# New times, priorities, load order and one engine choice for a chained attention, expert and channel-mix kernel

## The chip, the cores and the metric

The kernel runs on one core of a Trainium2 chip. The metric is device time in microseconds (us) of one execution; the profile shows one such execution of the kernel before. TensorE is called PE below, VectorE DVE, ScalarE ACT, GpSimd POOL, and SyncE SP; SP issues the transfers (DMAs).

## What is computed

Three layers follow each other, all in float32 (8 batches, 576 positions, width 512):

```python
p_packed = sm_attn(p, k, v)              # 32 packed queries look at 576 keys, 8 heads of 64
out = sm_attn(q, p_packed, p_packed)     # 576 queries look at the 32 packed rows
...
for e in range(E):                       # 4 experts, causal attention of width 64, top 2 by gate
    q = x @ wq[e]; k = x @ wk[e]; v = x @ wv[e]
    ...
    ye = a @ v @ wo[e]
    out += mask[..., None] * w[:, :, kk:kk + 1] * ye
...
xk = mu_k * x + (1.0 - mu_k) * x_prev    # x_prev: x shifted by one position
xr = mu_r * x + (1.0 - mu_r) * x_prev
k = np.maximum(xk @ w_k, 0.0)
v = k * k @ w_v
r = 1.0 / (1.0 + np.exp(-(xr @ w_r)))
return (r * v)
```

## The kernel before

**Precision.** A float32 product is made of three products of tiles that are split into a high and a low part (names ending in h and l): high by high, low by high, high by low.

**Phases.** From 0 to about 387 us the kernel runs the attention and the experts, batch after batch, and beside it folds the experts' output weights `wo` into the last layer's weights `w_r` and `w_k` (function `fold`, lines L693 to L791): each weight piece arrives as 64-bit words (`raw`), DVE, ACT and POOL turn it to float32 (`decode`), PE multiplies it (L777), and the folded weights go to DRAM (`wscr`). Of the four planes of a folded weight only two are stored; the other two are rebuilt when it is loaded. From 387 us `rstage` (L944) computes the r gate, from 459 us `kstage` (L964) the hidden layer, from 589 us `vunit` (L1005) the last product.

**What rebuilds a weight.** `load_weight` loads the two stored planes of `wr` (near the end of the expert phase), of `wk0` and of `wk1` (during `rstage`). For each of the two missing planes it subtracts (L864, 128x1024, into the single buffer `ws`), rounds to the high part on ACT (L865), and subtracts again for the low part on DVE (L866). The stored planes are split at L850 to L853.

**Steps and their times.** Each part of the work is a generator whose pieces ("steps") get a time from a table, in units of which a batch has 20: `front` (attention), `values`, `project` (L474, L487, L493: q, k of two experts), `soft` (L539 scores, L557 mask and row maximum on DVE, L561 exponential on ACT), `turn` (L586, L593: transposes), `pair_out` (L616 to L663: probabilities by values at L628, scaling `cs`, `cx`, `cb`, and `dt`, which goes to DRAM), `fold`, and the loads and stages of the last layer. The steps are sorted by time and written out in that order; a scheduler then fixes each engine's queue, with priorities (`PR`, `PR0`, `PR1`) that let a step's instructions go ahead. On the chip every engine works its queue strictly in order, and so does SP, on whose queue all DMAs stand: an instruction that waits holds all behind it.

**Shared buffers.** PSUM tiles come from two pools: `one` has four buffers, `big` two. A matmul into a `big` tile waits until the readers of the tile two before it are done. DMAs use eight semaphores in rotation, so each waits for the one eight before it. DMA `ms<-ms` (L570) moves the 64x64 corner `mq` of an expert's scores between the buffers, and L593 transposes it.

**The opening.** `load_first` issues the first loads in the order of `LOADS` (`k`, `v`, `q` with the head group, `wo`, `r` for a raw weight piece, `wa` for the experts' input weights). `FILL` adds 128x64 matmuls that only keep PE working.

Of the kernel before, what the change touches and what calls it, by code (L numbers as in the profile page):

```python
# [20 lines left out]

FRONT_T = [-29.98, -26.81, -23.33, -16.88, -17.51, -14.04, -12.67, -12.1, -8.35]
G1_T = [1.16, 2.59, 3.23, 1.72, 1.63, 8.19, 3.77, 1.61, 3.2]
OPEN_T0 = [-29.98, -26.81, -23.33, -16.88, -17.51, -14.04, -12.67, -12.1, -8.35]
OPEN_T1 = [-28.82, -24.22, -20.1, -15.16, -15.88, -5.85, -8.9, -10.49, -5.15]
VAL_T = [-3.35, 0.36, -1.9, 0.35, 0.62]
PROJ_T = [-2.04, -1.82, 1.38, 2.56]
GROUPS = ((0, 3), (1, 2), (4,))  # L30
SOFT_T = [1.76, 1.75, 2.48]
TURN_LAG = [4.78, 4.58, 5.02]
OUT_LAG = [3.59, 5.08, 7.48]
FOLD_0 = [-21.99, -18.2, -16.87, -12.45, -10.56, -6.17, -3.87, -1.05, -0.52, 1.63, 3.63, 7.17, 8.98]
FOLD_T = [5.65, 105.86]
LOADS = 'k0 k1 v0 q0 wo r r v1 q1 wa'
LATE1 = [0.0, 0.0]
TIES_V, TIES_A = [0, 1, 2, 2], [0, 0, 1, 1]
FILL = [[0, 0, 0, 0, 0, 0], [0, 0, 0, 0, 0, 0]]
Q_MOVE = 'SSSS'  # L40
SLOTS = 2
E_SLOT = 'V'
E_HALF = 'D'
SMALL0 = 'VV'
SEQ = ''
PR0, WARM = (1000, 946, 1043, 1073, 1037, 1000, 940, 980, 907), 16
PR1 = [990, 936, 1033, 1063, 1027, 990, 930, 970, 897]
WR_AT = 7.41
R_LOAD, R_RUN = ([15.69, 16.11], [22.66, 28.61])
W_AT = [5.5, 5.2]  # L50
K_AT = [(0, -1.0, 0)] + [(0, 0.0, j) for j in range(4)] + [(1, -1.0, 0)] + [(1, 0.0, j) for j in range(5)]
E_TURN = "VAAAA"
E_DIAG = "AAAAV"
E_TURN2 = "AAAAA"
E_DIAG2 = "AAAVA"
E_WH, E_SQ, E_B, E_G, E_CXL = "P", "A", "V", "V", "A"
E_AT, E_VG, E_CB, E_PT, E_PPT, E_CX = "A", "A", "A", "V", "A", "V"
E_Z = "P"
E_DT, E_WL = "P", "P"
PR = {'front': 0, 'values': -100, 'project': 0, 'soft': 0, 'turn': 0, 'out': 236, 'fold': 0, 'k': 46, 'gates': 0}  # L60


def f32(ap):
    return ap.bitcast(F32)
# [3 lines left out]
def kernel(  # L68
# [83 lines left out]
    if True:  # L152
# [41 lines left out]
        def zeros():  # L194
            for t in kls:
                nc.gpsimd.memset(f32(t[64:, 0, :]), 0.0)
                nc.gpsimd.memset(f32(t[:64, 1, :]), 0.0)
            yield
            for x, t in enumerate(mss):
                nc.gpsimd.memset(t, 0.0)  # L200
                if x < len(tbs):
                    nc.gpsimd.memset(rowap(tbs[x][64:, :64], TS + P, NT, 64), 0.0)
                yield

        def halves(ap):
            return ap.rearrange("p (h n) -> p h n", h=2)
# [4 lines left out]
        def evac(eng, o, x):  # L211
            if eng == "A":
                return nc.scalar.copy(o, x)  # L213
            if eng == "V":
                return nc.vector.tensor_copy(o, x)
            return pool_copy(o, x)
# [56 lines left out]
        def load_first():  # L273

            got = {}
            first["raw"] = []
            for x in LOADS.split():
                if x == "wa":
# [15 lines left out]
        def fill(b, g, x, ps, o, ins):  # L294


            for _ in range(0 if b else FILL[g][x]):
                with tc.issue_after(ins.ins):
# [162 lines left out]
        def project(b, ep):  # L461
# [5 lines left out]
            for x in range(2):  # L467
# [17 lines left out]
                if x == 0:  # L485
                    nc.scalar.copy(halves(z[:, 0, :]), pv)
                    nc.vector.tensor_sub(halves(l), pv, halves(f32(z[:, 0, :])))  # L487
                    evac(E_Z, z[64:, 1, :], f32(z[64:, 0, :]))
                else:
# [18 lines left out]
        def rowap(base, stride, n, w):  # L508
            return bass.AP(
                tensor=base.tensor, offset=base.offset, ap=[base.ap[0], [stride, n], [1, w]]  # L510
            )
# [64 lines left out]
        def turn(b, e, group):  # L576
# [17 lines left out]
            for i, o in blocks:  # L594
                if i:
                    q0 = i * P - TAIL
                    evac(
                        (E_TURN if b < 4 else E_TURN2)[i], rowap(tb[:, q0 : q0 + P], TS, i, P),
                        ps[:, o : o + i * P].rearrange("p (j q) -> p j q", q=P),
# [3 lines left out]
            evac(  # L603
                (E_DIAG if b < 4 else E_DIAG2)[i],
                rowap(tb[:64, (TS + P) * i : (TS + P) * i + 64], step, ng, 64),
# [210 lines left out]
        def call(fn, *args):  # L816
            fn(*args)
            yield
# [36 lines left out]
        def load_weight(n_, eng):  # L855
            h, l = wres[n_]
            for j in range(SLOTS):
                fetch(f32(l[:, j]), wscr[n_][:, j], True)
            yield
            sub = (nc.vector if E_SLOT == "V" else nc.gpsimd).tensor_sub  # L860
            if SLOTS < NS:
                w = pools["a"].tile([P, 2, 512], F32, tag="ws", name=nm("ws"), bufs=1)
                for j, x in ((2, l[:, 0]), (3, w)):
                    pin(sub(w, f32(x) if j == 2 else x, f32(l[:, 1])))  # L864
                    pin(nc.scalar.copy(h[:, j], w))  # L865
                    pin(nc.vector.tensor_sub(l[:, j], w, f32(h[:, j])))  # L866
                    yield
            for j in range(SLOTS):
                split_late(h[:, j], l[:, j], eng)
                yield  # L870

        def swap_end():

            close(sm_cm, vp_cm, ex_cm, bt_cm)
            cms["b"], pools["b"] = pool("bb", 1, "left")
            for n_ in ("k0", "k1"):
                weight(n_, "b")
                yield from load_weight(n_, "AV" if n_ == "k0" else "AP")
            wres["v"] = [
                pools["b"].tile([P, NFT, DM], F32R, name="wv" + x, bufs=1) for x in "hl"  # L880
            ]
            yield
# [130 lines left out]

        last = U * (B - 1) + max(t + max(0, d) for t, d in zip(FRONT_T, G1_T)) + 0.1
        prio = {}

        def add(kind, gen, times, prior=None):
            prio[gen] = PR[kind] if prior is None else prior
            for t in times:
                steps.append((t, gen))  # L1020

        def even(t0, t1, n):
            return [t0 + (t1 - t0) * i / n for i in range(n)]

        add("front", zeros(), [-6.0 + 0.5 * i for i in range(6)])
        add("fold", fold(), FOLD_0 + even(FOLD_T[0], FOLD_T[1], NFOLD - len(FOLD_0)))
        swap = max(last, FOLD_T[1] + 0.1)
        add("k", call(swap_w), [swap])
        add("k", load_weight("r", "PV"), [swap + WR_AT - 2.0] + even(swap + WR_AT + 1.0, swap + WR_AT + 5.0, 4))
        end = U * B + OUT_LAG[2] + 0.1  # L1030
        for i in range(NEB):
# [149 lines left out]
```

## Time and profile before

| | us |
|---|---|
| median of 3 runs (lowest, highest) | 795.42 (792.72, 796.65) |
| the profiled execution, own time | 790.75 |
| its span | 789.0 |
| PE busy in it | 755.3 (96%) |
| DVE, ACT, POOL busy | 478.5, 453.1, 357.7 |

The span is the time from the first to the last instruction on the core; 1.75 us of the execution's own time lie around it. PE's mean granted clock is 0.978 of full speed.

### The profile page before, as it was taken

The page shows a single profiled execution, that of the slowest core. Times are in us where ns is not written, and L with a number is a line of the kernel's source. Part 1 is how long each engine was busy: PE and PEld are TensorE (multiplying, and loading weights), DVE is VectorE, ACT ScalarE, POOL GpSimd, SP SyncE. Part 2 cuts the span into 40 slices and gives each one's busy share as a digit, 9 for nine tenths or more (in the row PEclk, how much of TensorE's full clock was granted, in tenths as well). Part 3 has the DMA queues.
Part 4 walks back from the last instruction along what each step waited for, and adds up shares of the span by engine and source line. Part 5 has one row for each costly group of instructions (what it writes and reads, how often), then busy time and mean ns, then how long its engine had stood idle before and what let it go on. Part 6 is the DMA issues. An engine that isn't in the chain of part 4 may idle for free.

```text
span 789.0 us, 15325 instructions
## 1 busy us (share of the span) xinstructions
PE 755.3 (96%) x5504; PEld 622.3 (79%) x5504; DVE 478.5 (61%) x1182; ACT 453.1 (57%) x1031; POOL 357.7 (45%) x456
## 2 busy tenths in 40 slices
PE   6788989999999999999899999999999999999998
PEld 4486967879697887877778888888888888888886
DVE  3977886988868668777757978887581111111111
ACT  2367757678767769687633442422968756555400
POOL 7357657664766715252501063631267443433600
PEclk8599999999999999999899999999999999999999
DMA  9955463545636353215358686857889565555411
GB/s 317 302 152 169 129 182 116 170 152 160 197 111 175 116 143 109 71 37 147 118 187 287 227 265 203 292 190 236 322 279 338 170 188 172 181 181 158 135 65 54
DMA packets 88460, 142.06 MB, mean 180 GB/s; under 512 B 9280, under 2 KB 60992, under 8 KB 86080
## 3 DMA queue, kind: packets, MB, share of 16 engines
q1 hardware_dynamic: 88240, 141.07, 56.3%
q8 instruction: 44, 0.72, 0.4%
q14 instruction: 32, 0.26, 0.1%
q10 hardware_dynamic: 144, 0.00, 0.0%
HBM read 83.90 MB, written 47.19 MB: 166 GB/s over the span
## 4 chain that ended last, share of the span: by engine, by line
PE 78%; DMA 7%; DVE 7%; ACT 3%; POOL 2%; issue 1%; SPq 1%; DVEq 0%; ACTq 0%; POOLq 0%
PE one L1005 25%; PE one L964 8%; PE big L964 8%; PE big L474 6%; PE one L628 5%; PE one L944 4%; PE big L944 4%; PE one L777 4%; PE one L419 3%; PE one L539 2%; PE one L586 2%; DMA raw<-in_w_k_dram 2%; DMA ms<-ms 2%; PE big L244 2%; PE big L539 1%
## 5 line engine op out<-in xcount | busy, mean ns | idle before, releaser
L1010 DVE TENSOR_TENSOR ring<-one,ring 128x512 f32<-128x512 f32 x36 | 24.9, 692 | 167.8 <-PE one L1005 158.5
L1005 PE MATMUL one<-wvh,yh 128*128 128x512 f32 x288 | 112.0, 389 | 0.0
L1005 PE MATMUL one<-wvl,yh 128*128 128x512 f32 x288 | 112.0, 389 | 0.0
L1005 PE MATMUL one<-wvh,yl 128*128 128x512 f32 x288 | 112.0, 389 | 0.0
L561 ACT ACTIVATE ms<-ms,nb 128x192 f32<-128x192 f32 (+3 forms) x128 | 78.5, 617 | 19.1 <-DVE nb L557 18.6
L219 POOL TENSOR_TENSOR yl<-yvh,yh 128x1024 fp32r<-128x1024 f32 (+1 forms) x24 | 49.1, 2060 | 44.3 <-ACT yh L990 26.3
L213 ACT COPY tb<-one 64x128 f32<-64x128 f32 (+5 forms) x208 | 61.7, 362 | 10.9 <-PE one L593 9.9
L708 POOL TENSOR_TENSOR dcx<-dcx,dcu 128x256 f32<-128x256 f32 x40 | 29.9, 747 | 83.3 <-DVE dcu L702 61.2
L1005 PEld LDWEIGHTS one<-wvh,yl 128*128 128x128 f32 x288 | 54.1, 188 | 11.3
L1005 PEld LDWEIGHTS one<-wvh,yh 128*128 128x128 f32 x288 | 54.1, 188 | 11.2
L1005 PEld LDWEIGHTS one<-wvl,yh 128*128 128x128 f32 x288 | 54.1, 188 | 11.1
L219 POOL TENSOR_TENSOR yl<-yvl,yh 128x1024 fp32r<-128x1024 f32 x16 | 38.2, 2398 | 39.5 <-ACT yh L990 17.1
L628 PE MATMUL one<-tb,vg 128*64 128x320 f32 (+4 forms) x448 | 54.6, 372 | 0.4 <-DVE nb L557 0.4
L586 PE MATMUL one<-ident,ms 128*128 128x128 f32 x320 | 53.6, 281 | 0.5 <-ACT ms L561 0.2
L557 DVE CUSTOM_DVE_ANT_0 ms<-one,mstrip 128x192 f32<-128x192 f32 (+2 forms) x96 | 43.3, 480 | 14.0 <-PE one L539 13.5
L628 PEld LDWEIGHTS one<-tb,vg 128*64 128x64 f32 x448 | 35.8, 140 | 17.1 <-issue 1.9
L219 POOL TENSOR_TENSOR dt<-cb 128x192 f32<-128x192 f32 (+1 forms) x48 | 29.7, 648 | 35.1 <-DMA dl<-dscr 20.9
L586 PEld LDWEIGHTS one<-ident,ms 128*128 128x128 f32 x320 | 36.8, 142 | 10.1 <-ACT ms L561 6.0
L1128 ACT ACTIVATE ring<-ring 128x1024 f32<-128x1024 f32 x18 | 19.1, 1061 | 35.6 <-DMA ring<-rscr 35.6
L539 PE MATMUL one<-ks,qs 128*128 128x192 f32 (+3 forms) x128 | 36.9, 302 | 1.5 <-ACT tb L213 1.1
L539 PE MATMUL one<-kl,qs 128*128 128x192 f32 (+3 forms) x128 | 35.3, 309 | 0.0
L729 POOL TENSOR_TENSOR wl<-wc,wh 128x256 fp32r<-128x256 f32 x48 | 34.6, 746 | 0.4
(218 smaller groups left out, 2046.9 us busy)
## 6 DMA issues: line engine op xcount, KB each, us to landing
yscr<-y SPq DMA_DIRECT2D x48, 384.0 KB, 3.6
dl<-dscr SPq DMA_DIRECT2D x40, 256.0 KB, 4.9
yvh<-yscr SPq DMA_DIRECT2D x10, 1024.0 KB, 5.6
kT<-in_k_dram SPq DMA_DIRECT2D x16, 576.0 KB, 4.1
qT<-in_q_dram SPq DMA_DIRECT2D x16, 576.0 KB, 5.0
rscr<-rr SPq DMA_DIRECT2D x12, 768.0 KB, 4.3
ring<-rscr SPq DMA_DIRECT2D x36, 256.0 KB, 2.9
out_dram<-ring SPq DMA_DIRECT2D x36, 256.0 KB, 3.2
```

Source lines behind the costliest of these rows:

```text
L213: return nc.scalar.copy(o, x)
L219: nc.gpsimd.tensor_tensor(o, x, y, op=op)
L474: nc.tensor.matmul(ps[:, 512 * hf : 512 * hf + SH], ww[:, g, :], xx[:, g, :], start=i == 0, stop=i == 3 * NG - 1,)
L539: nc.tensor.matmul(ps[:, po : po + kn], qs[:, qo : qo + P], keys[:, ko : ko + kn], start=x == 0, stop=x == 1,)
L557: nc.vector.tensor_tensor_reduce(halves(mv) if last else mv, sv, halves(mk) if last else mk, op0=ALU.add, op1=ALU.min, scale=-SC, scalar=3 ...
L561: nc.scalar.activation(to, mv, AF.Exp, bias=nb[:n], scale=-1.0, accum_out=bat["sums"][:n, i, e : e + 1],)
L586: nc.tensor.transpose(ps[:, at + j * P : at + (j + 1) * P], ms[:, j * P : (j + 1) * P], ident)
L628: nc.tensor.matmul(av[64 * ee : 64 * ee + 64, qo - lo : hi - lo], vg[:, j, HD * (2 * ep + ee) : HD * (2 * ep + ee + 1)], tslice(tabs[ee], ...
L729: nc.gpsimd.tensor_sub(l, x, f32(h))
L944: nc.tensor.matmul(po, dx[:, NS * t + s, t0 : t0 + P], wpart("r", s, wx, t), start=n == 0, stop=n == 3 * KT - 1,)
L964: nc.tensor.matmul(po.rearrange("p (b n) -> p b n", b=2), wpart("k0" if f < 4 else "k1", s, wx, t)[:, f % 4 * P : f % 4 * P + P], dx[:, :, ...
L1005: nc.tensor.matmul(ps, a[:, f, P * t : P * t + P], wres["v"][b][:, f, :], start=n == 0, stop=n == 3 * NFT - 1,)
```

## The change

Nothing but the tables at the head of the file is edited (the lines that change only quote marks are left out here):

```diff
-FRONT_T = [-29.98, -26.81, -23.33, -16.88, -17.51, -14.04, -12.67, -12.1, -8.35]
+FRONT_T = [-30.21, -27.04, -23.56, -17.21, -17.74, -14.27, -12.9, -12.2, -8.58]
...
-PROJ_T = [-2.04, -1.82, 1.38, 2.56]
+PROJ_T = [-2.04, -1.53, 1.38, 2.59]
...
-LOADS = 'k0 k1 v0 q0 wo r r v1 q1 wa'
-LATE1 = [0.0, 0.0]
-TIES_V, TIES_A = [0, 1, 2, 2], [0, 0, 1, 1]
-FILL = [[0, 0, 0, 0, 0, 0], [0, 0, 0, 0, 0, 0]]
+LOADS = 'k0 k1 q0 wo v0 r v1 r q1 wa'
+LATE1 = [0.19, 0.3]
+TIES_V, TIES_A = [0, 1, 2, 2], [0, 0, 1, 0]
+FILL = [[0, 1, 0, 0, 0, 0], [0, 0, 0, 0, 0, 0]]
...
-E_SLOT = 'V'
+E_SLOT = 'P'
...
-WR_AT = 7.41
-R_LOAD, R_RUN = ([15.69, 16.11], [22.66, 28.61])
-W_AT = [5.5, 5.2]
+WR_AT = 7.79
+R_LOAD, R_RUN = [15.73, 16.13], [23.81, 28.91]
+W_AT = [5.49, 5.32]
```

`G1_T`, `OPEN_T0`, `OPEN_T1`, `VAL_T`, `TURN_LAG`, `OUT_LAG`, `FOLD_0`, `FOLD_T`, `PR0`, `PR1` and the priority `out` (236 to 387) change in the same way. `E_SLOT` moves the six subtractions L864 from DVE to POOL. One 128x64 matmul is added; otherwise the instructions are the same ones in another order. The order is the same on PE, DVE, ACT and POOL up to about the 53rd us of the profile, apart from that matmul; from there on each engine has moved rows in every batch.

The first place is DVE's queue during the first batch's `soft` steps (59 to 68 us in the profile). Before, the decoding of a raw weight piece (L693, L696) stands ahead of the second group's `PWl` (L378), which reads the `big` tile of that group:

```order
L693 TENSOR_SCALAR dce_1560<-raw_1557 128x256
L696 SCALAR_TENSOR_TENSOR dcx_1559<-raw_1557,dce_1560 128x256
L557 ISA ms_117,nb_146_866<-one_861,mstrip 128x448
L557 ISA nb_146_866 128x1
L557 ISA mq_869,nb_148_870<-one_861,mstrip 64x64
L557 ISA nb_148_870 64x1
L378 TENSOR_TENSOR PWl_378<-big_891,PWh_377 128x772
```

Now, in the queue of the changed kernel:

```order
L693 TENSOR_SCALAR dce_1584<-raw_1581 128x256
L381 TENSOR_REDUCE s_154_902<-st_813 128x9x2
L557 ISA ms_120,nb_143_855<-one_850,mstrip 128x192
L557 ISA nb_143_855 128x1
L557 ISA ms_116,nb_144_858<-one_850,mstrip 128x320
L557 ISA nb_144_858 128x1
L723 SCALAR_TENSOR_TENSOR wc_908<-dcq_986,dcx_983 128x256
L385 TENSOR_SCALAR r_155_904<-s_154_902 128x18
L557 ISA ms_117,nb_146_867<-one_862,mstrip 128x448
```

The decoding of that piece now stands at the head, before the row maxima; its L696, the 576-wide L557 and then `PWl` follow behind these rows. On SP the piece's load now stands ahead of the second `ks` and of `qT`, which it stood behind.

The second place is PE's queue at the end of the second pair's scores in the same batch (98 to 108 us). Before, the second `project` tile (L474 into big_1508) follows right behind the scores and transposes:

```order
L539 MATMUL big_1468<-ks_1315,qs_112 128x288
L539 MATMUL big_1468<-kl_114,qs_112 128x288
L539 MATMUL big_1468<-ks_1315,qs_112 128x288
L539 MATMUL big_1468<-kl_114,qs_112 128x288
L344 MATMUL one_1476<-vn_126,aT_234_1219 32x64 x8
L586 MATMUL one_1499<-ident,ms_116 128x128 x4
L593 MATMUL one_1504<-ident,ms_116 128x128
L474 MATMUL big_1508<-A2h,PWh_377 128x288 x2
```

Now:

```order
L586 MATMUL one_1500<-ident,ms_116 128x128 x4
L593 MATMUL one_1505<-ident,ms_116 128x128
L539 MATMUL big_1492<-ks_1316,qs_112 128x288
L539 MATMUL big_1492<-kl_114,qs_112 128x288
L539 MATMUL big_1492<-ks_1316,qs_112 128x288
L539 MATMUL big_1492<-kl_114,qs_112 128x288
L357 MATMUL one_1529<-ident,pp_1490 128x128
L628 MATMUL one_1539<-tb_125,vg_507 64x320
L474 MATMUL big_1509<-A2h,PWh_362 128x288 x2
```

The scores have moved behind the transposes, and a transpose of `pp` and a first L628 stand ahead of the project tile. The tile two before it in the pool is now another one, the source of an ACT copy.

The third place is POOL's queue at the end of the expert phase (359 to 391 us). Before:

```order
L209 TENSOR_SCALAR qs_113<-qs_113 64x576
L457 COPY gws_5753<-gw_5744 64x4
L219 TENSOR_TENSOR dt_5895<-cb_5890 128x2x192
L219 TENSOR_TENSOR dt_5895<-cb_5890 128x192 x2
L852 TENSOR_SCALAR wrh_5575<-wrl_5576 128x1024 x2
L643 MEMSET cb_6068 128x1
L852 TENSOR_SCALAR dh_5577<-dl_5578 128x2x256 x6
L618 TENSOR_TENSOR cs_6040<-cs_6040,gws_5753 128x10
L852 TENSOR_SCALAR dh_5577<-dl_5578 128x2x256 x2
```

Now:

```order
L209 TENSOR_SCALAR qs_113<-qs_113 64x576
L864 TENSOR_TENSOR ws_5856<-wrl_5577 128x1024
L457 COPY gws_5752<-gw_5743 64x4
L864 TENSOR_TENSOR ws_5856<-ws_5856,wrl_5577 128x1024
L219 TENSOR_TENSOR dt_5896<-cb_5891 128x2x192
L219 TENSOR_TENSOR dt_5896<-cb_5891 128x192 x2
L852 TENSOR_SCALAR wrh_5576<-wrl_5577 128x1024 x2
L643 MEMSET cb_6069 128x1
L852 TENSOR_SCALAR dh_5578<-dl_5579 128x2x256
L618 TENSOR_TENSOR cs_6041<-cs_6041,gws_5752 128x10
L852 TENSOR_SCALAR dh_5578<-dl_5579 128x2x256 x7
```

Both subtractions for `wr` have come in ahead of `dt`, and `cs` (L618) stands behind the first of the eight roundings of `dl`, where it stood behind the sixth.

## Rows read from the trace of the kernel before

**Rows 1.** Busy time in five stretches: engine, us busy (instructions), then PE clock, DMA.

```profile
0.00:120.00 120.00, 98.08 (x1064) 77.72 (x1065) 91.41 (x273) 66.11 (x177) 72.23 (x130) 0.89 0.66 210
120.00:360.00 240.00, 236.16 (x2508) 197.72 (x2507) 180.97 (x589) 178.22 (x537) 130.63 (x213) 1.00 0.45 129
360.00:388.00 28.00, 24.02 (x160) 19.27 (x159) 23.97 (x60) 19.71 (x61) 12.89 (x16) 0.88 0.50 145
388.00:460.00 72.00, 72.00 (x345) 58.78 (x344) 53.49 (x73) 30.44 (x55) 7.28 (x10) 1.00 0.61 212
```

**Rows 2.** Opening, timeline of PE (start, us busy), then stretches as in rows 1.

```profile
16.20 1.30 PE L344 MATMUL one<-vn,aT 128*32 128x64 f32 x40 [3.01 <-DMA vn<-in_v_dram]
...
16.00:38.00 22.00, 15.68 (x163) 8.64 (x164) 19.69 (x46) 7.95 (x15) 9.28 (x15) 0.50 0.96 332
```

**Rows 3.** Timelines of DVE and PE around 65 us, then one stretch.

```profile
64.64 0.37 DVE L693 TENSOR_SCALAR dce<-raw 128x256 int32<-128x256 int32 x1 [1.49 <-DMA raw<-in_w_k_dram]
...
67.25 0.72 PE L244 MATMUL big<-qT,ppT 64*32 64x288 f32 x16 [2.19 <-DVE PWl L378]
...
68.00:76.00 8.00, 8.00 (x84) 6.25 (x86) 8.00 (x27) 7.20 (x23) 4.10 (x6) 1.00 0.44 131
```

**Rows 4.** Timelines of PE and DVE around 103 us, then stretches.

```profile
103.35 0.53 PE L474 MATMUL big<-A2h,PWh 128*128 128x288 f32 x2 [3.20 <-DVE nb L557]
...
102.53 0.76 DVE L557 CUSTOM_DVE_ANT_0 ms<-big,mstrip 128x576 f32<-128x576 f32 x1
...
104.00:106.00 2.00, 2.00 (x11) 1.98 (x10) 0.65 (x2) 0.20 (x2) 1.51 (x3) 0.51 0.56 158
106.00:108.00 2.00, 2.00 (x13) 1.41 (x13) 1.20 (x3) 1.75 (x4) 0.34 (x1) 0.64 0.05 14
113.00:126.00 13.00, 11.97 (x118) 8.24 (x118) 11.93 (x40) 12.05 (x40) 6.19 (x7) 1.00 0.64 212
```

**Rows 5.** End of the expert phase, timeline of PE, then one stretch.

```profile
372.67 0.33 PE L593 MATMUL one<-ident,ms 128*128 128x128 f32 x1 [1.26 <-DMA ms<-ms]
...
385.68 0.77 PE L639 MATMUL big<-ident,cx 128*128 128x128 f32 x5 [1.38 <-ACT cx L213]
...
387.36 0.71 PE L944 MATMUL big<-wrh,dh 128*128 128x512 f32 x2
...
374.00:380.00 6.00, 5.79 (x23) 4.36 (x24) 6.00 (x17) 5.63 (x19) 1.37 (x3) 0.50 0.95 297
```

**Rows 6.** The same time on POOL, DVE, ACT and SP's DMA queue.

```profile
368.47 1.82 POOL L219 TENSOR_TENSOR dt<-cb 128x384 f32<-128x384 f32 x3 [5.62 <-DVE cb L646]
...
370.26 3.03 POOL L852 TENSOR_SCALAR wrh<-wrl 128x1024 fp32r<-128x1024 f32 x2
...
379.87 4.40 POOL L852 TENSOR_SCALAR dh<-dl 128x512 fp32r<-128x512 f32 x4 [2.63 <-DMA dl<-dscr]
384.23 0.64 POOL L618 TENSOR_TENSOR cs<-cs,gws 128x10 f32<-128x10 f32 x1
...
366.15 1.22 DVE L864 TENSOR_TENSOR ws<-wrl 128x1024 f32<-128x1024 f32 x1
...
372.66 1.70 DVE L864 TENSOR_TENSOR ws<-ws,wrl 128x1024 f32<-128x1024 f32 x1
...
368.54 1.07 ACT L865 CAST wrh<-ws 128x1024 fp32r<-128x1024 f32 x1
...
371.50 0.54 SPq L663 DMA_DIRECT2D dscr<-dt  x1
```

**Rows 7.** POOL's 128x1024 subtractions: page group, and its timeline in `rstage`.

```profile
L219 POOL TENSOR_TENSOR yl<-yvh,yh 128x1024 fp32r<-128x1024 f32 (+1 forms) x24 | 49.1, 2060 | 44.3 <-ACT yh L990 26.3
...
457.12 4.98 POOL L853 TENSOR_TENSOR wk1l<-wk1l,wk1h 128x1024 fp32r<-128x1024 f32 x2 [40.60 <-ACT wk1h L850]
```

**Rows 8.** End of `wk0`'s rebuilding on DVE, and its first use on PE.

```profile
447.93 1.22 DVE L853 TENSOR_TENSOR wk0l<-wk0l,wk0h 128x1024 fp32r<-128x1024 f32 x1
...
458.53 0.62 PE L964 MATMUL one<-dh,wk0h 128*128 128x512 f32 x2
```

More of the change, by code (lines that the diff above doesn't have):

```diff
@@ L20 @@
 EPS = 1e-9
-FRONT_T = [-29.98, -26.81, -23.33, -16.88, -17.51, -14.04, -12.67, -12.1, -8.35]
[L25 to L28, printed above, removed]
-PROJ_T = [-2.04, -1.82, 1.38, 2.56]
+FRONT_T = [-30.21, -27.04, -23.56, -17.21, -17.74, -14.27, -12.9, -12.2, -8.58]
+G1_T = [1.28, 2.71, 3.35, 1.84, 1.55, 8.03, 3.89, 1.73, 3.32]
+OPEN_T0 = [-30.24, -27.07, -23.59, -17.14, -17.77, -14.3, -13.93, -12.36, -8.71]
+OPEN_T1 = [-28.21, -23.61, -19.69, -14.48, -15.27, -5.24, -8.29, -9.88, -4.54]
+VAL_T = [-3.35, 0.49, -1.9, 0.35, 0.62]
+PROJ_T = [-2.04, -1.53, 1.38, 2.59]
 GROUPS = ((0, 3), (1, 2), (4,))
 SOFT_T = [1.76, 1.75, 2.48]
[L32 to L35, printed above, removed]
-LOADS = 'k0 k1 v0 q0 wo r r v1 q1 wa'
-LATE1 = [0.0, 0.0]
-TIES_V, TIES_A = [0, 1, 2, 2], [0, 0, 1, 1]
-FILL = [[0, 0, 0, 0, 0, 0], [0, 0, 0, 0, 0, 0]]
+TURN_LAG = [4.82, 4.32, 5.06]
+OUT_LAG = [3.75, 5.26, 7.66]
+FOLD_0 = [-21.71, -17.92, -12.7, -11.98, -10.19, -5.7, -3.4, -0.41, -0.13, 2.75, 5.36, 8.87, 10.68]
+FOLD_T = [6.14, 106.01]
+LOADS = 'k0 k1 q0 wo v0 r v1 r q1 wa'
+LATE1 = [0.19, 0.3]
+TIES_V, TIES_A = [0, 1, 2, 2], [0, 0, 1, 0]
+FILL = [[0, 1, 0, 0, 0, 0], [0, 0, 0, 0, 0, 0]]
 Q_MOVE = 'SSSS'
 SLOTS = 2
-E_SLOT = 'V'
+E_SLOT = 'P'
 E_HALF = 'D'
@@ L45 @@
 SEQ = ''
-PR0, WARM = (1000, 946, 1043, 1073, 1037, 1000, 940, 980, 907), 16
-PR1 = [990, 936, 1033, 1063, 1027, 990, 930, 970, 897]
-WR_AT = 7.41
-R_LOAD, R_RUN = ([15.69, 16.11], [22.66, 28.61])
-W_AT = [5.5, 5.2]
-K_AT = [(0, -1.0, 0)] + [(0, 0.0, j) for j in range(4)] + [(1, -1.0, 0)] + [(1, 0.0, j) for j in range(5)]
[L52 to L60, printed above, removed]
+PR0, WARM = (1000, 946, 1043, 1073, 1037, 995, 940, 993, 907), 16
+PR1 = [990, 936, 1046, 1107, 1059, 869, 930, 942, 897]
+WR_AT = 7.79
+R_LOAD, R_RUN = [15.73, 16.13], [23.81, 28.91]
+W_AT = [5.49, 5.32]
+K_AT = [(0, -1.0, 0)] + [(0, 0.0, j) for j in range(4)] + [(1, -1.0, 0)] + [(1, 0.0, j) for j in range(5)]
+E_TURN = 'VAAAA'
+E_DIAG = 'AAAAV'
+E_TURN2 = 'AAAAA'
+E_DIAG2 = 'AAAVA'
+E_WH, E_SQ, E_B, E_G, E_CXL = 'P', 'A', 'V', 'V', 'A'
+E_AT, E_VG, E_CB, E_PT, E_PPT, E_CX = 'A', 'A', 'A', 'V', 'A', 'V'
+E_Z = 'P'
+E_DT, E_WL = 'P', 'P'
+PR = {'front': 0, 'values': -100, 'project': 0, 'soft': 0, 'turn': 0, 'out': 387, 'fold': 0, 'k': 46, 'gates': 0}
 def f32(ap):
```

## The prediction

> **What bounds the kernel now.** I read the stretches first, because they say where any time can be had at all. PE is busy for all of 388 to 460 us, and from there to the end the stages are the same instructions in the same arrangement; what is left is before 388 us [rows 1]. There PE is idle for 120 − 98.08 = 21.9 us up to 120, for 240 − 236.16 = 3.8 us from 120 to 360, and for 28 − 24.02 = 4.0 us from 360 to 388. The fourth column from the right end of these rows, PE's clock, shows a second loss: 0.89 and 0.88 of full speed in the first and third stretch, 1.00 in between.
>
> Then I read PE's timeline for the long waits and followed each to what released it. Four places matter:
>
> The opening: DMA share 0.96 from 16 to 38 us at 332 GB/s, the clock at 0.50, a 3.01 us wait for `vn` [rows 2]. It is bound by loads, and from 16 us DVE is busy 19.69 of 22 us as well.
>
> The 65th us: PE stands 2.19 us before L244, released by `PWl` on DVE. DVE had itself stood 1.49 us before the decoding of a raw piece, whose load came late; `PWl` was queued behind it [rows 3].
>
> The 100th to 103rd us: PE stands 3.20 us before the second project tile, until DVE has read the tile two before it (L557, 576 wide, at 102.53). That L557 stands behind gate copies on DVE. After this gap the clock is 0.51 for 2 us and 0.64 for 2 more [rows 4]: 2 × 0.49 + 2 × 0.36 = 1.7 us of work not done.
>
> The end of the phase: waits of 1.26 us for the corner DMA and 1.38 us for `cx`, and between them 5.79 us of PE work at clock 0.50, which costs 2.9 us [rows 5]. `cx` waits for `cs` on POOL, which at 384.23 stands behind six roundings of `dl` [rows 6].
>
> **The change part by part.** *Opening.* `v0` now comes after `q0` and `wo`, `v1` ahead of the second raw piece; the bytes ahead of `wa` are the same. One raw piece less before `v1` is 256 KB, at 332 GB/s an estimated 0.8 us of the 3.01 us wait; but behind it `wa` ends the next wait and still lands after the same bytes, and `v0`, later by `q0` and `wo`, may cost the first L344 as much. DVE, nearly full from 16 us, takes the rest. I take 0; bounds −0.8 and +0.8. The added 128x64 matmul stands in PE's wait for loads.
>
> *The 65th us.* The raw load stands two places earlier on SP, its decoding ahead of the row maxima on DVE, and the tile of L244 now follows a tile that the 576-wide L557 reads. `PWl` is needed one tile later. What is late next is that L557; nothing ahead of it on DVE waits for a load any longer, so I take −2.0 of the 2.19 us; bounds 0 (the load is late again) and −2.2.
>
> *The 103rd us.* The project tile now waits for an ACT copy long done instead of the L557; `pp`'s transpose and one L628 stand ahead of it. What could be late next is `pp` (L352 on DVE, behind the second L487) or the tile after. The full price is 3.20 + 1.7 = 4.9 us. Not all stays: DVE is busy 11.93 of 13 us from 113 to 126 and PE 11.97 [rows 4], so whatever DVE does not also do earlier comes back as a wait there. DVE's own queue gets shorter only by the 1.5 us that it stood at 64.6. I take −3.5; bounds −1 and −4.9.
>
> *120 to 360 us.* Every queue is reordered, and the six batches repeat one pattern. At most 3.8 us are to be had; the same reordering can open a wait as well as close one. I take 0; bounds −2 and +3.
>
> *End of the phase.* Three edits meet. (a) Two of the L864 leave DVE: 1.22 + 1.70 us less there [rows 6], beside the scores' maxima that PE waits for. (b) The transpose that waited for the corner DMA stands behind eight scores matmuls more: the 1.26 us goes, and with it perhaps the half clock. (c) `cs` is behind one rounding instead of six, five of some 1.1 us each (4.40 / 4): `cx` and the 1.38 us wait go. Together 1.26 + 1.38 + 2.9 = 5.5 us.
>
> Against them stands POOL's queue. A 128x1024 subtraction takes 2.06 us there, or 2.49 us in the form of L853 [rows 7]; L864 took 1.22 us on DVE. And both stand ahead of `dt`. The second must wait until the first's result has been rounded (1.07 us on ACT) and subtracted (1.22 us on DVE), since `ws` is one buffer: 2.06 + 1.07 + 1.22 + 2.06 = 6.4 us, at the earliest from 365 us on (DVE began at 366.15), so to about 371.5 to 373. `dt` (1.82 us) then ends at 373.5 to 375 instead of 370.3, its transfer leaves 2 to 3.5 us later than at 371.50, and behind it on SP stand the eight loads of `dl` on which the first `rstage` waits. They landed for the third rounding at 379.87; now for 382 to 383.5, with two more roundings and splits until L944 has its first operands at about 384.5 to 386. L944 began at 387.36 [rows 5]. So of the 5.5 us, 1.4 to 2.9 us can be kept at this place, whatever PE saves ahead of it. I take −2.5; bounds +1.5 (PE arrives early, waits, and the clock falls once more, as after the 1.26 us wait) and −5.
>
> On POOL beside DVE there is a further price. L864 took 1.70 us instead of 1.22 while POOL rounded `wrh` (370.26 for 3.03 us) [rows 6]. The Trainium skill says the same (GPSIMD Engine Reference, section 1): POOL's memory interfaces are shared with DVE, and DVE instructions with two SBUF inputs contend; section 4.1 advises elementwise work on VectorE, about twice as fast with two inputs. By that rule the move of the L864 is a loss. By the rows alone: twice 2.06 us on POOL, in which DVE would run at 1.22 / 1.70, costs 4.1 × 0.28 = 1.2 us of DVE, less than the 2.92 us it is relieved of.
>
> *`rstage`.* Four L864 for `wk0` and `wk1` go to POOL as well, which is idle for 40.60 us there [rows 7]. Each is 0.9 to 1.3 us longer; for `wk0` two of them, 2.5 us. Its last split ends at 447.93 + 1.22 = 449.15, and PE first uses `wk0` at 458.53 [rows 8]: 9.4 us of cover. I take 0. If the cover were gone, `kstage` would wait for the 2.5 us in full.
>
> The sum: 0 − 2.0 − 3.5 + 0 − 2.5 + 0 = −8.0 us. The profiled execution took 790.75 us, so 782.75, a ratio of 0.990. That execution lies 4.7 us under the median; by the same ratio the median of 795.42 becomes 787.4.
>
> **The rivals.** *Only moved (within 0.5%).* The waits at 65 and 103 us vanish and come back: DVE, 11.9 of 13 us busy from 113 to 126, sets the pace, and the end of the phase is held by `dl`. Then −2 or −3 remain: about 793. For it speaks that DVE has little slack in that stretch; against it that it has 16% or more in the first 120 us as a whole (91.41 of 120 busy).
>
> *POOL holds `rstage` (slower).* The chain L864, L865, L866, L864, `dt`, `dl` ends later than I count. The loads of `dl` left at 372; if DVE gets to the L866 between them 4 us later than I count, held by a maximum that waits for PE, `dl` is 6 to 7 us late instead of 2 to 3.5, L944 starts at 388.5 to 390 or later, and the gap is followed by 6 us at half clock, 3 us lost. The end then costs 1 to 2.6 us of lateness and 3 of clock instead of saving 2.5; with the two early places at their nearer bounds (0 and −1) the sum is +3 to +4.6, so about 799. It decides once the second L864 ends later than about 375. For it speaks the single buffer; against it that L866 stands directly ahead of the `cb` products on DVE, which PE needs early.
>
> *All closed (faster by more).* The waits at 120 to 360 us shrink by 2, the 103rd keeps its 4.9 and the end its 5: with the 2.2 that is −14, 781.5.
>
> *By the clock.* The Trainium skill (TensorE: Matmul & The Clock Gate, part 1) has activity release the clock and idleness throttle it. Here the 1.26 us wait was followed by half clock, the 2.19 us wait was not (1.00 from 68 to 76 us) [rows 3]. So the 1.7 and 2.9 us that I count as clock may stay though their waits go, or fall elsewhere: 4.6 us less saving, −3.4, 792.
>
> **How the numbers follow.** The forecast (−5 to −11) gets 0.45; all closed 0.13; only moved 0.17; the clock stays 0.12; POOL holds `rstage` 0.08; a reordered wait in 120 to 360 us that adds over 4 us 0.05. A measurement here tells about 0.5%, 4 us, from no change. Faster: 0.45 + 0.13 and a part of the clock case, 0.62. Slower: 0.08 and half of the last, 0.11. The same: 0.27. The range leaves out the slower tail above 797 and gains beyond 14 us: 780.5 to 797.
>
> **What would show it.** Right: no wait over 1 us at L244 near 65 us and at L474 near 100 us, clock 1.00 behind it; L639's wait for `cx` gone; L944 starting some 8 us earlier than at 387.36, and every later stage shifted by just that. Wrong: a wait of PE at the first L944 for `dh` or `dl`, POOL's `dt` starting past 375; new waits on DVE's L557 between 110 and 126; half clock in other places; PE waiting at the first L964.

## The result and the profile after

The changed kernel takes 786.75 us (median of 4 runs, 784.43 to 789.51) against 795.01 us for the kernel before (4 runs, 792.72 to 796.65): a ratio of 0.990, 95% interval 0.9858 to 0.9941. A second measurement, below, gave 0.9885. The profiled execution's span is 782.6 us, 6.4 us less than the 789.0 of the first trace; 789.0 − 8.0 = 781.0 had been forecast. The traced executions of both kernels (790.75 and 784.43 us) are the shortest that were timed of each, so a line of these traces need not stand for the median execution.

The stretches of the changed kernel, in the columns of [rows 1] (PE's clock is the third figure from the right, not the fourth as the prediction has it):

```profile
0.00:120.00 120.00, 102.38 (x1114) 80.55 (x1116) 98.14 (x289) 71.09 (x195) 74.89 (x133) 0.93 0.68 214
120.00:360.00 240.00, 234.15 (x2510) 198.78 (x2508) 179.63 (x590) 176.84 (x533) 127.37 (x211) 1.00 0.46 132
360.00:388.00 28.00, 23.14 (x143) 17.73 (x143) 20.46 (x50) 17.89 (x56) 20.99 (x22) 1.00 0.37 111
388.00:460.00 72.00, 72.00 (x342) 58.80 (x342) 53.72 (x64) 29.42 (x50) 20.12 (x12) 1.00 0.69 235
```

PE's idle time fell by 4.3 us before 120 us (21.9 to 17.6) and rose by 2.0 us between 120 and 360 and by 0.9 us from 360 to 388: together only 1.4 us. Between these two traces the rest of the gain is in the clock column: 0.93 for 0.89, and 1.00 for 0.88 at the end. Half clock is left in the opening alone. It is shorter there too, but that is worth little: PE's first scores (L539) begin at 45.86 us instead of 46.69, and in experiment 7, whose queues are the changed kernel's up to there, at 46.75.

The places of [rows 3, 4], PE's timeline of the changed kernel, and then the two stretches that were at half clock:

```profile
65.12 0.72 PE L244 MATMUL big<-qT,ppT 64*32 64x288 f32 x16
66.32 0.33 PE L593 MATMUL one<-ident,ms 128*128 128x128 f32 x1 [0.48 <-DMA ms<-ms]
...
99.46 0.53 PE L474 MATMUL big<-A2h,PWh 128*128 128x288 f32 x2
...
105.94 0.72 PE L244 MATMUL big<-qT,ppT 64*32 64x288 f32 x16 [0.38 <-DVE kl L493]
```

and the stretches:

```profile
104.00:106.00 2.00, 1.62 (x55) 1.23 (x58) 1.27 (x3) 1.27 (x2) 1.72 (x4) 1.00 0.65 168
106.00:108.00 2.00, 2.00 (x39) 1.25 (x40) 1.97 (x6) 0.60 (x1) 1.22 (x2) 1.00 0.81 186
```

L244 and L474 no longer wait; what is left nearby is under 0.5 us, and the clock stays at 1.00.

The end of the phase, [rows 5, 6]; timelines of PE, then of POOL, DVE and SP's queue:

```profile
363.36 0.40 PE L539 MATMUL big<-ks,qs 128*128 128x288 f32 x1 [0.96 <-ACT cb L213]
...
376.12 0.71 PE L639 MATMUL big<-ident,cx 128*128 128x128 f32 x5
...
379.11 0.73 PE L944 MATMUL big<-wrh,dh 128*128 128x512 f32 x2 [1.23 <-POOL dh L852]
...
380.66 0.73 PE L944 MATMUL big<-wrh,dl 128*128 128x512 f32 x2 [0.36 <-DVE dl L853]
...
359.20 2.36 POOL L864 TENSOR_TENSOR ws<-wrl 128x1024 f32<-128x1024 f32 x1 [5.32 <-DMA ms<-ms]
...
363.98 2.39 POOL L864 TENSOR_TENSOR ws<-ws,wrl 128x1024 f32<-128x1024 f32 x1 [2.31 <-DVE wrl L866]
366.32 1.80 POOL L219 TENSOR_TENSOR dt<-cb 128x384 f32<-128x384 f32 x3
...
362.67 1.23 DVE L866 TENSOR_TENSOR wrl<-ws,wrh 128x1024 fp32r<-128x1024 f32 x1 [2.51 <-ACT wrh L865]
...
368.15 0.38 SPq L663 DMA_DIRECT2D dscr<-dt  x1
```

The chain L864, L865, L866, L864, `dt` stands there as written down: the second L864 waits 2.31 us for DVE, `dt` ends at 368.12, and its transfer leaves at 368.15. The batch's work ahead of it (a block of 26 L628 that began at 341.77 before and at 335.81 now) is 6.0 us earlier, the transfer only 371.50 − 368.15 = 3.4 us. So `dt` is 2.6 us late in its batch, and PE waits 1.23 and 0.36 us at the first L944 for `dh` and `dl`. The waits for `cx` and of 1.26 us for the corner transfer are gone.

The first L944 begins 8.25 us earlier than the 387.36 of [rows 5], but not every later stage is shifted by that: the first L964 begins at 451.68, 6.85 us earlier, and the span is 6.4 us shorter. Four scores matmuls (L539, from 381.80) that stood ahead of the first L944 now stand behind it.

What came back lies at the corner transfer. Of the changed kernel, PE's largest such wait, the transfer's issue, and the summary of waits from 0 to 400 us (us in total, times, longest):

```profile
250.94 0.33 PE L593 MATMUL one<-ident,ms 128*128 128x128 f32 x1 [2.52 <-DMA ms<-ms]
...
245.55 0.47 SPq L570 DMA_DIRECT2D ms<-ms  x1
```

```profile
PE one L593 <- DMA ms<-ms: 4.7, 5, 2.5
```

The 16 KB transfer took some 5 us; the loads of `vn` and `qT` had been issued just ahead of it and another `qT` right behind.

### The profile page after: what moved, and what is told of

Same layout as the page of the kernel before. It is cut to its first block, busy times and chain, and to the rows that moved or that the text cites. A ratio compares the mean times of both kernels' runs of the same rounds, so it can differ in the third digit from the quotient of the medians.

```text
span 782.6 us, 15327 instructions
## 1 busy us (share of the span) xinstructions
PE 750.4 (96%) x5506; PEld 618.9 (79%) x5506; DVE 475.5 (61%) x1176; ACT 451.4 (58%) x1031; POOL 374.8 (48%) x462
## 4 chain that ended last, share of the span: by engine, by line
PE 68%; DVE 11%; DMA 10%; ACT 4%; POOL 3%; issue 2%; SPq 1%; DVEq 0%; POOLq 0%; ACTq 0%
PE one L1005 24%; PE big L964 5%; PE one L964 5%; PE one L628 5%; PE big L474 5%; PE one L944 4%; PE big L944 4%; PE one L777 3%; PE one L419 3%; PE one L586 2%; DMA ms<-ms 2%; DMA raw<-in_w_k_dram 2%; PE one L539 2%; DMA yscr<-y 2%; DVE ms L557 1%
## 5 line engine op out<-in xcount | busy, mean ns | idle before, releaser
L628 PE MATMUL one<-tb,vg 128*64 128x320 f32 (+4 forms) x448 | 52.6, 362 | 0.5 <-DVE nb L557 0.4
L557 DVE CUSTOM_DVE_ANT_0 ms<-one,mstrip 128x192 f32<-128x192 f32 (+2 forms) x96 | 43.6, 483 | 15.3 <-PE one L539 14.0
L628 PEld LDWEIGHTS one<-tb,vg 128*64 128x64 f32 x448 | 34.5, 136 | 16.6 <-issue 1.4
L539 PE MATMUL one<-ks,qs 128*128 128x192 f32 (+3 forms) x128 | 36.8, 302 | 0.5 <-DMA ks<-ks 0.4
L539 PE MATMUL one<-kl,qs 128*128 128x192 f32 (+3 forms) x128 | 34.9, 306 | 0.0
```

Source lines behind the costliest of these rows:

```text
L539: nc.tensor.matmul(ps[:, po : po + kn], qs[:, qo : qo + P], keys[:, ko : ko + kn], start=x == 0, stop=x == 1,)
L557: nc.vector.tensor_tensor_reduce(halves(mv) if last else mv, sv, halves(mk) if last else mk, op0=ALU.add, op1=ALU.min, scale=-SC, scalar=3 ...
L628: nc.tensor.matmul(av[64 * ee : 64 * ee + 64, qo - lo : hi - lo], vg[:, j, HD * (2 * ep + ee) : HD * (2 * ep + ee + 1)], tslice(tabs[ee], ...
```

## The experiments

**Theory A**, the prediction's: each place gives its own part, as the order there decides. **Theory B**: the clock differs between executions, whatever the order. **Theory C and D**: parts closed in one place come back in another, or pay only together. Each kernel was timed against the kernel before on the same chip; experiments 1 to 4, 5 to 8 and 9 to 12 ran on three different chips, so kernels of different groups are compared by their ratios. In sum:

| kernel | median us | before | ratio | 95% interval |
|---|---|---|---|---|
| changed kernel again | 786.90 | 795.54 | 0.9885 | 0.9851 to 0.9919 |
| opening's tables alone | 791.61 | 795.54 | 0.9948 | 0.9924 to 0.9973 |
| batch tables alone | 796.32 | 795.54 | 0.9994 | 0.997 to 1.0018 |
| end's tables alone | 794.84 | 795.54 | 0.9991 | 0.9972 to 1.001 |
| opening and batch | 790.99 | 796.00 | 0.9941 | 0.9919 to 0.9962 |
| batch and end | 791.47 | 796.00 | 0.9949 | 0.9929 to 0.9969 |
| changed, L864 back on DVE | 791.90 | 796.00 | 0.9956 | 0.9935 to 0.9976 |
| changed, corner by POOL | 789.65 | 796.00 | 0.9942 | 0.9919 to 0.9965 |
| first loads and `FILL` alone | 795.33 | 796.77 | 0.9986 | 0.9962 to 1.0009 |
| L864 on POOL alone | 792.80 | 796.77 | 0.9958 | 0.9934 to 0.9982 |
| changed, corner sent by ACT | 801.32 | 796.77 | 1.0063 | 1.0039 to 1.0088 |

From the stretches of 2 us of each trace I worked out PE's idle time (2 − busy, summed) and the work lost to the clock (busy × (1 − clock), summed), in us; the clock's loss up to 60 us (5.7 to 9.1 us) is left out, as the first scores begin at 45.4 to 46.8 us in all these traces:

| trace | L864 on | idle 60–80 | 100–120 | 120–360 | 360–400 | clock 60–120 | 120–360 | 360–400 |
|---|---|---|---|---|---|---|---|---|
| before | DVE | 2.3 | 4.2 | 3.8 | 4.0 | 1.7 | 0 | 3.3 |
| before again | DVE | 3.2 | 4.0 | 5.5 | 6.5 | 1.6 | 0 | 1.3 |
| changed | POOL | 0.8 | 0.9 | 5.8 | 4.9 | 0 | 0 | 0 |
| changed again | POOL | 0.7 | 0.9 | 5.1 | 4.7 | 0 | 0 | 0 |
| opening alone | DVE | 3.5 | 2.1 | 5.1 | 5.1 | 0 | 0 | 4.1 |
| batch alone | DVE | 2.3 | 1.9 | 6.6 | 7.0 | 0 | 1.7 | 1.6 |
| end alone | POOL | 2.3 | 3.2 | 6.1 | 4.4 | 3.0 | 0 | 0 |
| opening and batch | DVE | 2.3 | 0.8 | 7.1 | 6.0 | 0 | 0 | 3.1 |
| batch and end | POOL | 2.3 | 2.2 | 6.7 | 3.9 | 0 | 0 | 0 |
| changed, L864 on DVE | DVE | 0.7 | 0.8 | 6.3 | 5.0 | 0 | 1.7 | 3.3 |
| corner by POOL | POOL | 1.1 | 0.2 | 6.1 | 4.6 | 0 | 0 | 0 |
| first loads alone | DVE | 2.8 | 4.4 | 5.8 | 6.9 | 1.4 | 1.7 | 1.6 |
| L864 on POOL alone | POOL | 2.8 | 3.6 | 6.0 | 4.0 | 3.1 | 0 | 0 |
| corner sent by ACT | POOL | 3.6 | 3.1 | 13.1 | 2.5 | 1.6 | 4.5 | 0 |

**1. The opening's tables alone.** In the kernel before:

```diff
-FOLD_0 = [-21.99, -18.2, -16.87, -12.45, -10.56, -6.17, -3.87, -1.05, -0.52, 1.63, 3.63, 7.17, 8.98]
-LOADS = 'k0 k1 v0 q0 wo r r v1 q1 wa'
+FOLD_0 = [-21.71, -17.92, -12.7, -11.98, -10.19, -5.7, -3.4, -0.41, -0.13, 2.75, 5.36, 8.87, 10.68]
+LOADS = 'k0 k1 q0 wo v0 r v1 r q1 wa'
```

with `OPEN_T0`, `OPEN_T1`, `LATE1`, `TIES_A`, `FILL`, `PR0` and `PR1`; of these only `FOLD_0`, `LOADS` and `FILL` move a row in the queues.

> The kernel before with the tables of the opening alone (OPEN_T0, OPEN_T1, LOADS, TIES_A, FILL, PR0, PR1, FOLD_0, LATE1). Theory A (each place gives its own part, and the parts add): the wait of PE at the 65th us goes (1.5 to 2.2 us), the opening gives up to 0.8 us, the waits at 103 us, 373 and 386 us and the half clock behind them stay: ratio about 0.997 (-2 to -3 us). Theory B (the gain is the clock, which falls or not from one execution to the next whatever the order): no difference, ratio 1.000. Theory C (waits closed here only open others behind them): no difference in time, but the 65th us is closed and PE stands longer between 100 and 130 us.

−0.52%, about 4.1 us: more than Theory A's 2 to 3. PE's timeline:

```profile
66.23 0.72 PE L244 MATMUL big<-qT,ppT 64*32 64x288 f32 x16 [1.25 <-DVE PWl L378]
...
73.60 0.72 PE L628 MATMUL one<-tb,vg 128*64 128x320 f32 x2 [1.29 <-DVE nb L557]
...
102.31 0.53 PE L474 MATMUL big<-A2h,PWh 128*128 128x288 f32 x2 [1.19 <-DVE nb L557]
```

The wait at 65 us is 0.9 us shorter and comes back at L628: PE's idle time from 60 to 80 us is 3.5 us, where it was 2.3. But the wait at 102 us, which Theory A gave to the batch tables, fell from 3.20 to 1.19 us, and the half clock behind it is gone.

**2. The batch tables alone** (`FRONT_T`, `G1_T`, `VAL_T`, `PROJ_T`, `TURN_LAG`, `OUT_LAG`, `FOLD_T`):

```diff
-PROJ_T = [-2.04, -1.82, 1.38, 2.56]
+PROJ_T = [-2.04, -1.53, 1.38, 2.59]
```

> The kernel before with the batch tables alone (FRONT_T, G1_T, VAL_T, PROJ_T, TURN_LAG, OUT_LAG, FOLD_T). Theory A: the 3.20 us wait at 103 us and the 1.7 us of half clock behind it go, some 2 us come back between 120 and 360 us as a wait for the corner transfer in the fifth or sixth batch; the 65th us keeps its wait and the end keeps its 1.3 us waits and its half clock: -2 to -4 us, ratio 0.995 to 0.997. Theory B: the half clock appears or not irrespective of the waits; about -1.5 us from the waits alone. Theory C: nothing.

No difference (0.9994), where A expected 0.995 to 0.997. In the trace the waits at L244 near 65 us and at L474 near 100 us are closed to under 0.8 us each and the half clock behind the second is gone; from 60 to 80 us PE is idle for 2.3 us all the same, 1.08 us of it at an L777 behind L557. Time is given back at the corner transfers:

```profile
257.56 0.33 PE L593 MATMUL one<-ident,ms 128*128 128x128 f32 x1 [2.91 <-DMA ms<-ms]
```

the longest of them, and in the summary of waits:

```profile
PE one L593 <- DMA ms<-ms: 9.6, 8, 2.9
```

with 1.7 us of half clock behind it.

**3. The end's tables alone.**

```diff
-E_SLOT = 'V'
-WR_AT = 7.41
+E_SLOT = 'P'
+WR_AT = 7.79
```

with `R_LOAD`, `R_RUN`, `W_AT` and the priority `out`.

> The kernel before with the tables of the end alone (WR_AT, R_RUN, R_LOAD, W_AT, the priority out, and E_SLOT on POOL). Theory A: all is as before up to 360 us; then the waits for the corner transfer and for cx go, a wait of about 1.5 us at the first L944 for the rounded dl comes, and the half clock from 374 to 380 us goes with the 1.26 us wait: -2 to -3 us, ratio about 0.997. Theory B: the half clock is as likely as before; then -0 to +1 us. Theory C: the wait at the first L944 takes everything back, ratio 1.000 or over.

The ratio was 0.9991: not the expected 2 to 3 us. Of A's end, no wait for `cx`, a corner wait no more and no half clock from 360 to 400 us came out. The wait at the first L944 for `dl` was 0.3 us, not 1.5; one of 1.85 us at L539 for ACT's `cb` opened. And the k stage now waited for DVE (0.89 and 0.36 us at L964, 0.41 at the last L944). And the trace bears on B: the queues up to 360 us are those of the kernel before, the wait at L244 is the same 2.19 us, and this time the clock fell behind it (PE's timeline, then the stretch of 2 us):

```profile
67.87 1.22 PE L244 MATMUL big<-qT,ppT 64*32 64x288 f32 x16 [2.19 <-DVE PWl L378]
```

```profile
68.00:70.00 2.00, 2.00 (x25) 0.51 (x31) 2.00 (x7) 1.57 (x7) 1.04 (x3) 0.50 0.00 0
```

**4. The changed kernel again.**

> The changed kernel once more, for a second trace. Theory A: the order decides where the clock falls, so that behind 40 us no stretch at half clock of more than 2 us is seen again, and the ratio is 0.990 again. Theory B: the clock differs between executions of one kernel; stretches at half clock appear at other places in this trace, and PE's idle time alone is like in the first trace.

As A: no half clock behind 40 us in this trace either, idle times within 0.8 us of the first in each stretch. But this execution (784.51 us) is again the shortest of its measurement, and like the first it has a mean granted clock of 0.989. The eight executions of the changed kernel that were not traced have 0.973 to 0.987 and took 785.58 to 789.68 us. So the two traces do not rule out B for them.

**5. Opening and batch, 6. batch and end.** The changed kernel with the tables of the end, or of the opening, as before.

> The changed kernel with the tables of the end as before (WR_AT, R_LOAD, R_RUN, W_AT, the priority out, L864 on DVE). Theory A (the parts add): the opening alone gave -4.1 us and the batch tables alone -0.5 us, so -4.6 us, ratio 0.994. Theory D (a part pays only where the others keep what it gained): the end keeps its waits for the corner transfer and for cx and its half clock, which the three end edits alone removed; without them 3 to 5 of the 8.6 us are lost, ratio 0.993 to 0.996. The two differ only in the trace: by D the time gained before 360 us is 6 us or more and is given back at the end; by A it is 4.6 us or less.

> The changed kernel with the opening's tables as before. Theory A (the parts add): -0.5 - 0.7 = -1.2 us, ratio 0.9985. Theory D: the batch tables closed the waits at 65 and 103 us when alone and lost it again at 257 us and at the end; with the end's tables the latter is kept, so -4 to -5 us, ratio 0.994 to 0.995.

0.9941 and 0.9949. The first is A's sum (0.9948 × 0.9994 = 0.9942), and its trace is A's too: the L593 that waits 1.26 us begins at 369.60, 3.1 us earlier than the 372.67 of [rows 5]. The end is the old one, with 3.1 us lost to half clock:

```profile
369.60 0.33 PE L593 MATMUL one<-ident,ms 128*128 128x128 f32 x1 [1.26 <-DMA ms<-ms]
...
382.41 1.33 PE L639 MATMUL big<-ident,cx 128*128 128x128 f32 x5 [1.62 <-ACT cx L213]
```

The second came out as D expected; but D's premise, that the end's edits need the batch's, falls with experiment 11.

**7. L864 back on DVE.** The changed kernel with

```diff
-E_SLOT = 'P'
+E_SLOT = 'V'
```

> The changed kernel with the six L864 back on DVE. Theory P (POOL's chain holds the first r stage): dt leaves 2 to 3.5 us earlier, the wait of PE at the first L944 for dh (1.23 and 0.80 us in two traces) goes, DVE's 2.4 us of L864 lie where it has slack: faster by 0.5 to 1.5 us than the changed kernel, ratio 0.987 to 0.989. Theory R (relief of DVE): the row maxima wait behind L864 again, waits of over 1 us and half clock come back between 365 and 385 us: slower by 2 to 4 us, ratio 0.992 to 0.995.

0.9956, against 0.990 and 0.9885 with POOL: 4.5 to 5.6 us slower. The time is Theory R's, and Theory P fell. All the waits that the end had before are back, though the late tables are the new ones:

```profile
368.96 0.33 PE L593 MATMUL one<-ident,ms 128*128 128x128 f32 x1 [1.26 <-DMA ms<-ms]
...
382.26 0.77 PE L639 MATMUL big<-ident,cx 128*128 128x128 f32 x5 [2.73 <-ACT cx L213]
...
456.25 0.73 PE L944 MATMUL big<-wrh,dh 128*128 128x512 f32 x2 [1.86 <-DVE rr L929]
```

and behind the second, in stretches:

```profile
384.00:386.00 2.00, 2.00 (x7) 1.67 (x7) 2.00 (x6) 1.00 (x4) 0.20 (x1) 0.50 0.00 0
```

The last wait is new: in `rstage` too the rebuilding of `wk1` on DVE (an L864, then an L866 of 2.47 us at 452.59) stands ahead of a combination (L929) that PE waits for.

The way is not quite R's. What stands directly ahead of the corner's maximum on DVE is not an L864 but the L866 that follows one (366.41, 1.56 us); and on POOL `cs` stands behind six roundings of `dl` again. So the edit works in part through the order that the scheduler makes of it. No run moves the L864 and keeps all other rows in their places, so the relief of DVE and the new order are not told apart.

**8. The corner by POOL**, and **12. the corner sent from ACT's queue.** The changed kernel with

```diff
-E_HALF = 'D'
+E_HALF = 'P'
```

and with `'A'` there.

> The changed kernel with the 64x64 corner copied by POOL instead of a transfer (32 copies). Theory E (the corner transfer waits behind the loads of values and queries, and its wait is what the batches give back): the waits at L593 for it, 4.7 us in the first trace, go; POOL gets about 32 times 0.3 us of work more: faster by 2 to 4 us, ratio 0.984 to 0.987. Theory F: POOL's queue, in order and fuller, holds the copies and other things behind them; the waits at L593 stay, released by POOL: ratio 0.989 to 0.995.

> The changed kernel with the corner transfers issued from ACT's queue instead of SP's. Theory E (the transfer is slow because the loads of values and queries run at the same time): it lands as late, waits at L593 remain at 4 to 6 us, ratio 0.988 to 0.991. Theory H (SP's queue holds its issue): the waits go, 2 to 4 us faster than the changed kernel, ratio 0.984 to 0.987.

Both have a higher ratio than the changed kernel, 0.9942 (the two intervals meet at 0.9919) and 1.0063. By POOL all waits for the transfer go, and the idle time from 120 to 360 us stays at 6.1 us, now for ACT's `tb` and DVE's maxima, with 1.51 us for POOL's copy at the end: Theory F. Sent from ACT, the waits at L593 grow:

```profile
122.56 0.33 PE L593 MATMUL one<-ident,ms 128*128 128x128 f32 x1 [3.49 <-DMA ms<-ms]
```

and in the summary:

```profile
PE one L593 <- DMA ms<-ms: 10.7, 6, 3.5
```

Neither E nor H expected that. Both edits also reorder the queues, so the cost of the transfer itself stays unmeasured.

**9. The kernel before again.**

> The kernel before once more, for a second trace: its first one (span 789.0 us) was faster than nearly all of its executions. Theory A (order decides): the same waits at 65, 103, 373 and 386 us with the same half clock behind the 3.20 us and the 1.26 us wait, and none elsewhere. Theory B (the clock differs between executions): the same waits within 0.3 us, half clock behind others of them (the 2.19 us wait for instance), and a longer span by what the clock takes.

Of both: the same waits (3.09 instead of 2.19 us at L244, 3.18 at L474, 1.25 and 2.16 at the end), half clock again behind L474, none behind the 3.09 us. At the end it moved: none behind the 1.25 us wait, which half clock followed in the first trace, but half clock from 386 us, behind 1.64 us at another L593 and at the 2.16 us wait for `cx`. The span was 793.6 us, 4.6 us more than that of the trace on which the prediction rests.

**10. First loads and `FILL` alone.**

> The kernel before with the new order of the first loads and the added 128x64 matmul alone; the queues of DVE, ACT and POOL are unchanged. Theory A (DVE's chain and the loads bound the opening): 0 to -0.8 us, ratio 0.999 to 1.000, and the 4.1 us of the opening's tables come from the fold steps (FOLD_0) that they move. Theory G (the opening's loads are worth more): PE reaches its first scores at 46 us more than 1.5 us earlier and about half of the 4.1 us is here, ratio 0.997 to 0.998.

0.9986, an interval that holds 1 and 0.997. The trace is nearer to A: PE's first scores begin at 46.28 us instead of 46.69, 0.4 us earlier, where G wanted more than 1.5. By the medians the other 0.38% of the opening's tables, about 3 us, is `FOLD_0`; the intervals of experiments 1 and 10 overlap.

**11. L864 on POOL alone**, all tables as before:

```diff
-E_SLOT = 'V'
+E_SLOT = 'P'
```

> The kernel before with the six L864 on POOL alone. Theory P (POOL's move is what reorders the end; the late tables do little): as with all the end's edits alone, -0.7 us, ratio 0.998 to 1.000: the waits for the corner transfer and cx go, and a wait of 1 to 2 us for DVE appears in the k stage. Theory T (the late tables do it): the waits at the end stay, POOL's chain delays the first r stage: +1 to +3 us, ratio 1.001 to 1.004.

0.9958, −3.3 us: Theory P in kind and more than it in size. PE waits 1.31 us for `cb` instead, as in the changed kernel (0.96). The waits for `cx` and of 1.26 us for the corner are gone with none of the late tables touched; the k stage waits 0.26 us. Why the late tables beside it (experiment 3) lose this gain, in which the k stage's waits of 1.25 us have a part, stays open; the two intervals overlap.

## Why the prediction came out

*The sum* was −8.0 us and came out as −8.3. *Its terms* were not all where I had put them, and that the sum is so near is in part luck: what was sized too low and what was lost elsewhere nearly cancel, and the two traces differ by 6.4 us only. By the medians, the opening's tables alone (0.52%), the batch tables alone (0.06%) and the move to POOL alone (0.42%) sum to 1.0%, the changed kernel's gain.

*The opening*, taken as 0 with bounds of 0.8: the loads give 0.14%, some 1.1 us, not told from nothing. Whether DVE or the loads set the pace there no run separates.

*The 65th us* (−2.0) and *the 103rd* (−3.5): in the traces both waits and the half clock behind the second went, as said, 1.5 and 3.4 us of idle time and 1.7 us of clock; the 103rd is 5.1 us in all, 1.6 more than I took. The step that failed is whom the 103rd was put down to. I gave it to the new order of `project`; experiment 1 leaves `PROJ_T` as it was and still shortens it to 1.19 us, without half clock. The batch tables close it by themselves too, but gain nothing in the median (0.9994), and adding them to the opening adds 0.07%. No run has the opening's and the end's tables without the batch tables.

The 65th does go with the earlier load and decoding of the raw piece, as I said. They come with `FOLD_0`, not with `LOADS`: in experiment 10 DVE still waits 1.94 us for that piece and PE 2.64 us at L244. But `FOLD_0` alone does not lower the idle time there, and the new order does not hold by itself: in experiment 5 DVE waits 1.32 us for the raw piece at 62.47, and PE is idle for 2.3 us from 60 to 80 us, against 0.7 in experiment 7, which has the same order of DVE's rows there. That the load is late again was my bound of 0; it comes in some executions.

*120 to 360 us*, taken as 0 with bounds −2 and +3: +2.0 us of idle time, at the corner transfer that I had counted only where it stood before. "Only moved" was right here in kind.

*The end* (−2.5): 0.42% with the move to POOL alone, 3.3 us, so of the right size, though 0.09% with all of the end's tables alone. The brake I had worked out was there: `dt` 2.6 us late in its batch (2 to 3.5 forecast), 1.6 us of waits at the first L944. But I had counted three edits, the move to POOL as a price and partly a relief, the new places of the transpose and of `cs` as the gain. By experiments 5, 7 and 11 the move carries all of it: with L864 on DVE the late tables give nothing (0.9956 with them, 0.9941 without), and with L864 on POOL the rows move by themselves, since the scheduler fills DVE's queue differently. The changed kernel with L864 on POOL and the old late tables was not run.

*The price on POOL*: L864 took 2.36 to 2.41 us there, 3.32 once, where I had taken 2.06. The Trainium skill's advice (GPSIMD Engine Reference, section 4.1) to keep such work on VectorE holds for the instruction, 1.22 us on DVE; for this kernel the measurement decides the other way, by the 0.42% of experiment 11.

*By the clock* is what the traces leave open. Between the first two traces PE's idle time fell by only 1.4 us up to 388 us, and the 5.0 us of work that half clock took behind 60 us are gone; I had given that a chance of not coming. But both traces of the changed kernel are its shortest executions, with the highest granted clock (0.989; 0.978 in the trace of before). At the same mean clock the gain is no smaller: five executions of the changed kernel at 0.973 to 0.980 took 785.58 to 789.51 us, the 62 of the kernel before in that range 792.3 to 802.59. Where half clock lay in them no trace shows. So a higher clock is not shown to be most of the median's gain, and how that gain splits into waits and clock stays open.

*`rstage`* was hidden as forecast: PE has no idle time from 388 to 460 us.

## What to carry to other kernels

Where PE's queue hangs on one other engine, the worth of a move is not the moved instruction's two durations but also what its place in the queue holds up: six moves of 1.2 us on DVE to 2.4 us on POOL paid 3.3 to 5.6 us. Undo each table of a retuned kernel by itself before crediting a place to it: two sets of tables here shorten the same wait at L474, and only one of them gains. And compare the time and the granted clock of a traced execution with those of the others: a wait's half clock came in one trace and not in another, and two traces of the shortest executions do not show the median one.

## What the hardware showed that I had not expected

The same wait is not always followed by half clock. The same 2.19 us wait in the same queues was followed by a clock of 1.00 once and 0.50 once; 2.64 us by full clock in experiment 10 and half in experiment 11; 3.09 us by full clock. The wait of 3.2 us at L474 was followed by half clock in all five traces that have it. The changed kernel is not safe from it either: behind its corner wait of 2.52 us at 250.94 the clock stayed at 1.00, but in experiment 7, whose queues up to there are the changed kernel's, the same L593 waits as long and the stretch behind it is at half clock:

```profile
252.05 0.33 PE L593 MATMUL one<-ident,ms 128*128 128x128 f32 x1 [2.53 <-DMA ms<-ms]
...
254.00:256.00 2.00, 2.00 (x21) 0.58 (x21) 2.00 (x9) 2.00 (x6) 0.35 (x1) 0.50 0.00 0
```

At the end of the phase the kind of the waits tells more than their sum. The seven traces with L864 on POOL have 2.5 to 4.9 us of idle time from 360 to 400 us and lose nothing to the clock; the seven with L864 on DVE have 4.0 to 7.0 us and lose 1.3 to 4.1 us each. In the changed kernel the idle time there is more than in the first trace of before (4.9 against 4.0), in pieces of 1.23 us at most; but experiment 3, with L864 on POOL, has a piece of 1.85 us and full clock. What keeps the clock up there was not tried by itself.
